# One turned dV or dK tile a block, loads before stores on the queue, and new places for the heads' borrowed-bank work

## The chip, the cores and the metric

The kernel runs on one core of one Trainium2 chip. Time is what the device takes for one execution, in microseconds (us). The times of a kernel are the median of several runs; a profile is one further execution, recorded by the hardware profiler. Times inside a profile are counted from the start of its span.

## The reference, cut to what matters

The reference is a forward pass and its gradient. With `x` of 2048 rows and 576 columns, 32 heads of width 128, and a feed-forward width of 4608, the forward pass is

```python
def _A_ref(x, k_cache, v_cache, wq, wo):
    q = (x @ wq).reshape(B, Sq, H, Dh).transpose(0, 2, 1, 3)
    scores = jnp.einsum("bhqd,bhkd->bhqk", q, k_cache) * (Dh ** -0.5)
    p = _softmax(scores, axis=-1)
    o = jnp.einsum("bhqk,bhkd->bhqd", p, v_cache)
    return o.transpose(0, 2, 1, 3).reshape(B, Sq, H * Dh) @ wo

def _B_ref(x, w_gate, w_up, w_down):
    g = jnp.einsum("bsd,df->bsf", x, w_gate)
    u = jnp.einsum("bsd,df->bsf", x, w_up)
    return jnp.einsum("bsf,fd->bsd", _sigmoid(g) * u, w_down)

xn = _layernorm(x)
out = x + _A_ref(xn, k_cache, v_cache, wq, wo) * _silu(_B_ref(xn, w_gate, w_up, w_down))
```

The kernel returns `out` and, for a given gradient of `out`, the gradients of `x`, `k_cache` (dK), `v_cache` (dV), `wq`, `wo`, `w_gate`, `w_up` and `w_down`. All arrays are bfloat16.

## The kernel before, in words

The work runs through stages on five engines: TensorE (PE) multiplies, VectorE (DVE) and ScalarE (ACT) take results out of the accumulators (PSUM) and do the elementwise work, GpSimd (POOL) does smaller elementwise work and issues DMAs, SyncE (SP) only issues DMAs. What SyncE issues goes out in its program order: an entry that waits holds back all that follow.

- **Feed-forward forward pass** (0 to 463 us): layer norm, gate and up products, down product. Its rows go to scratch arrays in DRAM (`h_d`, `a_d`, `b_d`).
- **Heads** (463 to 3665 us, 32 of them). The order of TensorE, DVE and ACT is written out by hand: every step of a head gets a place on a scale on which one head is 64 places long (`HEAD`), and steps are sorted by place (`at`, `anchor`). The scores of a query tile (`s_half`, two halves of 1024 keys), its exponential on ACT (`s_exp`, L563, a slab `Pq` of 128x2048), the product of dO and V (`dp_half`) and the slab `dSq` fill a head's frame. Each slab is turned by a transposing DMA on SyncE (L600, `PT` and `dST`), except the `dSq` of query tile 9, which TensorE turns in two halves of eight transposes (`trans_pe`, places `DST_PE` after the tile's own). Row products (`row_mm`, L612) read the turned slabs, `kv_mm` (L630) reads slabs as they are and accumulates dV and dK transposed, half of the keys at a time: VA, VB, KA, KB, at places found by filling the frame evenly (`level`), from 24 to 86.7, so into the next head's frame.
- **Borrowed banks.** `ps_acc` has four PSUM banks. `kv_mm` holds two of them for a whole half of the keys (`acckv`), `row_mm` one (`acc`). The rest of the heads' work takes what is left: projections of QT and dOT (`proj`, L511: four chunks of five steps, 0.4 places apart, evicted by ACT) and groups of eight transposes (`pe_transposes`, L518: KT, VT, dOn, Qn and the turned `dSq`, evicted by ACT or DVE). Their places are `QT_AT`, `DOT_AT`, `KT_AT`, `DON_AT`, `VT_AT`, `QN_AT` and `DST_PE` (L684 to L686). QT and KT are those of the next head.
- **Output product and dO** (3665 to 3801 us, L852).
- **Dh stage** (3801 to 4406 us): 18 blocks of 256 feed-forward columns. Per block: dh (L905), `du_blk` and `dg_blk` from it, dWdown (L923), dWup and dWgate (L947, L955). `load_abh(fb + 2)` loads the block after next: `a_blk` and `b_blk` on SyncE (L885), which wait until this block's elementwise work has read their slots, and `h_blk` on POOL. `load_wdT` loads, in pieces, the next third of the turned `w_down`, needed from blocks 6 and 12.
- **c2** (4406 to 4676 us): eight groups of four heads, dWo (L1005) and dWq (L1014, L1023), from `onb` and `dqb`, loaded two groups ahead.
- **c4** (4676 us to the end): the gradient of x, eight groups of 256 rows. Per group eight passes over chunks that transposing DMAs bring (L1061): six chunks `cf` in three slots and two chunks `cq` in two slots.

**The turned tiles.** The heads write dV and dK transposed to DRAM (`dvT_d`, `dkT_d`), 64 tiles of 128x2048 (512 KB each). Later stages turn them back: a transposing DMA loads a tile into SBUF, a plain DMA stores it. `turn(pool, n)` first issues the stores of the tiles loaded last, then loads `n` tiles. Every pool has two slots.

```python
    def turn(pool, n):
        while turned:
            nc.sync.dma_start(*turned.pop(0))
        for _ in range(n):
            if turns:
                ...
                nc.sync.dma_start_transpose(t_[:], src)
```

The dh stage turns two tiles a block (36), c2 two a group (16), c4 the last 12, one in each of passes 1, 4 and 7 of groups 1 to 4.

Of the kernel before, what the change touches and what calls it, by code (L numbers as in the profile page):

```python
# [9 lines left out]
bf = mybir.dt.bfloat16  # L10
# [3 lines left out]
P = 128  # L14
# [81 lines left out]
def kernel(  # L96
# [6 lines left out]
    nc = tc.nc  # L103
    cfg = dict(cfg or {})
    _, S, D = A_x.shape
    _, H, Sk, Dh = A_k_cache.shape
# [3 lines left out]
    NT = S // P  # L110
# [37 lines left out]
    turns = [(src[h], out[0, h].rearrange("(p t) d -> p t d", t=NT)) for h in range(H) for src, out in ((dkT_d, out_2), (dvT_d, out_3))]  # L148
    turned = []

    def turn(pool, n):
        while turned:
            nc.sync.dma_start(*turned.pop(0))
        for _ in range(n):
            if turns:
                src, dst = turns.pop(0)
                t_ = pool.tile([P, NT, P], bf, name="turn")
                nc.sync.dma_start_transpose(t_[:], src)
                turned.append((dst, t_[:]))


# [262 lines left out]
    with tc.tile_pool(name="ld2", bufs=2) as ld2, tc.tile_pool(name="ld1q", bufs=1) as ld1q, \  # L424
# [258 lines left out]
        KVE, OUE = "ss", "s"  # L683
        WOT_AT, DST_PE = 2.0, (6.3, 8.2)  # L684
        QT_AT, DOT_AT = ((41.4, 46.7, 50.0, 53.8), "s"), ((5.6, 8.6, 13.4, 17.4), "s")
        KT_AT, DON_AT, VT_AT, QN_AT = (45.5, 49.2, "s"), (16.2, 25.4, "v"), (29.6, 31.2, "s"), (33.6, 39.4, "s")  # L686
        PSTEP = 0.4
# [101 lines left out]
    if True:  # L789
# [19 lines left out]
        with tc.tile_pool(name="c1b", bufs=1, side="right", reuse_waits="tile") as blk, \  # L809
# [26 lines left out]
            def load_wdT(i, k=0):  # L836
                nc.sync.dma_start_transpose(wdT_h[k][:, i, :], B_w_down[k * FH:(k + 1) * FH, dlo[i]:dlo[i] + P])
# [32 lines left out]
        with tc.tile_pool(name="b1o", bufs=2, reuse_waits="tile") as outp, tc.tile_pool(name="b1k", bufs=2, reuse_waits="tile") as tkp, tc.tile_pool(name="b1t", bufs=3, reuse_waits="tile") as tmpp, \  # L870
# [21 lines left out]
            for fb in range(F // FB):  # L892
# [41 lines left out]
                else:  # L934
                    make_dh()
                    for fl in range(FB // P):
                        make_dwd(fl)
                load_abh(fb + 2)
                if fb < DT * (NWD - 1):
                    load_wdT(fb % DT, 1 + fb // DT)  # L940
                turn(tkp, 2)
                for (blk_, out_, nm) in ((du_blk, out_7, "dwu"), (dg_blk, out_6, "dwg")):
# [16 lines left out]
                for k, out_ in enumerate((out_7, out_6)):  # L959
                    nc.gpsimd.dma_start(out_[D - KL:, fcols], dwl[k * KL:(k + 1) * KL, :])  # L960
            turn(tkp, 0)
        pcw.release()
# [7 lines left out]
        with tc.tile_pool(name="c2b", bufs=1, reuse_waits="tile") as blk, tc.tile_pool(name="c2s", bufs=2, reuse_waits="tile") as sb, \  # L970
# [26 lines left out]
            for hg in range(NHG):  # L997
                cols = slice(hg * HG * P, (hg + 1) * HG * P)
                onb, dqb = held.pop(hg)
                for hl in range(HG):  # L1000
                    h = hg * HG + hl
                    accs = [ps.tile([P, 512], f32, name=f"acc{j}") for j in range(len(ncs))]
                    for st in range(NT):
                        for j, (n0, nn) in enumerate(ncs):
                            nc.tensor.matmul(accs[j][:, :nn], lhsT=onb[:, st, hl * P:(hl + 1) * P], rhs=ds_all[:, st, n0:n0 + nn],  # L1005
                                             start=(st == 0), stop=(st == NT - 1))
                    dwo = sb.tile([P, D], bf, name="dwo")
                    for j, (n0, nn) in enumerate(ncs):
                        alt.copy(dwo[:, n0:n0 + nn], accs[j][:, :nn])
                    nc.gpsimd.dma_start(out_5[h * P:(h + 1) * P, :], dwo[:])  # L1010
# [20 lines left out]
                for (dst, src, d0, kd) in wT_loads[2 * hg:2 * hg + 2]:  # L1031
                    nc.sync.dma_start_transpose(dst[:, :, d0:d0 + kd], src[d0:d0 + kd, :])
                turn(tkp, 2)
            turn(tkp, 0)

# [3 lines left out]
        with tc.tile_pool(name="c4c", bufs=1, reuse_waits="tile") as chp, tc.tile_pool(name="c4s", bufs=2, reuse_waits="tile") as sb, \  # L1039
# [11 lines left out]
            for sbi in range(S // SB2):  # L1051
# [7 lines left out]
                for pi, (src_d, wT, k0, KC, nm) in enumerate(passes):  # L1059
                    ch = chp.tile([P, KC, SB2], bf, name=f"cq{pi % 2}" if nm == "cq" else f"cf{pi % 3}")  # L1060
                    nc.sync.dma_start_transpose(ch[:], src_d[scol, k0 * P:(k0 + KC) * P])  # L1061
                    if sbi == 0 and pi in (1, 3, 4, 6):
                        load_wqT((1, 3, 4, 6).index(pi))
                    elif sbi and pi % 3 == 1:
                        turn(tkp, 1)
                    last = pi == len(passes) - 1
# [7 lines left out]
                for sl in range(nsl):  # L1074
# [23 lines left out]
                    (nc.sync if sbi == NSB - 1 else nc.gpsimd).dma_start(o1[rows, :], dx[:])  # L1098
            turn(tkp, 0)
            assert not turns  # L1100
# [32 lines left out]
```

## Time and profile before

| | us |
|---|---|
| median of 3 runs | 5077.68 (5071.66 to 5115.31) |
| the profiled execution, its own time | 5100.3 |
| its span | 5098.5 |
| TensorE busy | 4977.9 |
| chain that ended last: TensorE / DMA / issue | 86% / 8% / 2% |
| DMA, mean | 212 GB/s |

A line of the profile's groups names line, engine, operation, tiles (out<-in), shapes, count, then busy us and the mean ns of one, then the engine's idle time before it and what ended that. `SPq` is SyncE's queue of DMAs; the time beside an entry is how long SyncE was at it, its landing comes later. A busy TensorE need not be at its peak: a matmul counts as busy from its start to its modelled end, which overlaps the next one's start.

```profile
L612 PE MATMUL acc<-Kn,dST 128*128 128x128 bf16 x8192 | 977.0, 219 | 36.9 <-DMA dST<-dSq 36.2
...
L612 PE MATMUL acc<-Vn,PT 128*128 128x128 bf16 x8192 | 948.8, 219 | 11.7 <-DMA PT<-Pq 11.6
...
L630 PE MATMUL acckv<-Pq,dOn 128*128 128x512 bf16 x2048 | 762.9, 380 | 0.0
```

### The profile page before, as it was taken

Reading aid. Unit: us, or ns where it says so; the run is one execution under the profiler, and the core shown is the slowest. Engines: PE = TensorE matmul, PEld = TensorE weight load, DVE = VectorE, ACT = ScalarE, POOL = GpSimd, SP = SyncE. Lnnn points to the kernel's source line nnn. Section 1 sums busy time; section 2 is a strip of 40 time slices with the busy share of each in tenths; the row PEclk is TensorE's granted clock in tenths of the full one; section 3 lists DMA queues with packets and bytes.
Section 4 is the critical chain, followed back from the end, with each engine's and each line's share of the span. In section 5 each row is a group of like instructions: output and inputs, shape, how many; then the busy total and the mean of one; then the engine's idle time right before and its main releaser. Section 6 shows DMA issues by size and latency. Waiting matters only on the chain.

```text
span 5098.5 us, 103815 instructions
## 1 busy us (share of the span) xinstructions
PE 4977.9 (98%) x43024; PEld 3071.8 (60%) x43024; DVE 3087.7 (61%) x4821; ACT 2435.7 (48%) x3131; POOL 1484.0 (29%) x2197
## 2 busy tenths in 40 slices
PE   9999999999999999999999999999899999899999
PEld 3344666666666666666666666666457777654554
DVE  6556778878887887887888788777432222110101
ACT  5533656666666676666666667666202122100000
POOL 4322323333333333233333323322223223211000
PEclk9999999999999999999999999999999999999999
DMA  7889999999999999999999999999999999999995
GB/s 260 265 206 167 197 198 201 198 197 200 202 200 203 203 201 204 202 203 202 199 200 200 205 204 197 199 199 203 189 235 262 230 244 252 282 278 254 207 198 119
DMA packets 2855051, 1079.04 MB, mean 212 GB/s; under 512 B 2659889, under 2 KB 2782769, under 8 KB 2854577
## 3 DMA queue, kind: packets, MB, share of 16 engines
q1 hardware_dynamic: 2769312, 786.61, 87.3%
q0 software_dynamic: 85264, 285.79, 19.8%
q8 instruction: 336, 5.51, 0.4%
q14 instruction: 139, 1.13, 0.1%
HBM read 172.54 MB, written 234.55 MB: 80 GB/s over the span
## 4 chain that ended last, share of the span: by engine, by line
PE 86%; DMA 8%; issue 2%; DVE 2%; ACT 1%; POOL 1%; SPq 0%; DVEq 0%; POOLq 0%; ACTq 0%
PE acc L612 16%; PE acckv L630 15%; PE sp L552 8%; PE acc L1072 8%; PE dp L582 7%; PE accp L511 5%; PE accw L947 4%; DMA dST<-dSq 4%; PE dh L905 3%; PE acc L392 3%; PE accd L923 3%; PE acc L1005 3%; PE acc L852 2%; PE accq L1014 2%; PE acct L518 2%
## 5 line engine op out<-in xcount | busy, mean ns | idle before, releaser
L563 ACT ACTIVATE Pq<-sneg,nm 128x2048 bf16<-128x2048 bf16 x512 | 1025.0, 2002 | 182.6 <-DVE sneg L554 181.6
L585 DVE SCALAR_TENSOR_TENSOR dSq<-dp,delta,Pq 128x1024 bf16<-128x1024 f32 x608 | 774.9, 1282 | 445.9 <-PE dp L582 442.9
L612 PE MATMUL acc<-Kn,dST 128*128 128x128 bf16 x8192 | 977.0, 219 | 36.9 <-DMA dST<-dSq 36.2
L612 PEld LDWEIGHTS <-dST 128*128 128x128 bf16 x8192 | 692.3, 98 | 464.7 <-DMA dST<-dSq 57.6
L612 PE MATMUL acc<-Vn,PT 128*128 128x128 bf16 x8192 | 948.8, 219 | 11.7 <-DMA PT<-Pq 11.6
L612 PEld LDWEIGHTS <-PT 128*128 128x128 bf16 x8192 | 682.7, 98 | 428.8 <-DMA PT<-Pq 18.6
L630 PE MATMUL acckv<-Pq,dOn 128*128 128x512 bf16 x2048 | 762.9, 380 | 0.0
L630 PE MATMUL acckv<-dSq,Qn 128*128 128x512 bf16 x2048 | 758.9, 379 | 0.0
L554 DVE TENSOR_SCALAR_CACHE_REDUCE sneg<-sp,nm 128x1024 bf16<-128x1024 f32 x512 | 657.0, 1283 | 97.6 <-PE sp L552 64.8
L554 DVE TENSOR_SCALAR_CACHE_REDUCE sneg<-sp 128x1024 bf16<-128x1024 f32 x512 | 625.2, 1221 | 92.2 <-PE sp L552 82.8
L588 ACT ACTIVATE t<-dp,negdelta 128x1024 bf16<-128x1024 f32 x416 | 464.8, 1117 | 426.0 <-PE dp L582 324.5
L552 PE MATMUL sp<-KT,QT 128*128 128x512 bf16 x2048 | 610.5, 380 | 7.3 <-DVE sneg L554 7.0
L582 PE MATMUL dp<-VT,dOT 128*128 128x512 bf16 x2048 | 609.9, 379 | 0.6 <-DVE dSq L585 0.5
L592 DVE TENSOR_TENSOR dSq<-t,Pq 128x1024 bf16<-128x1024 bf16 x416 | 307.3, 739 | 0.0
L571 POOL TENSOR_TENSOR dOn<-dOn,rinv_all 128x256 bf16<-128x256 bf16 x256 | 153.8, 610 | 491.6 <-DVE dOn L42 305.4
L630 PEld LDWEIGHTS <-dOn 128*128 128x128 bf16 x2048 | 200.5, 98 | 74.5 <-issue 0.4
L630 PEld LDWEIGHTS <-Qn 128*128 128x128 bf16 x2048 | 200.5, 98 | 73.8
L511 PE MATMUL accp<-xnT,wq_h 128*128 128x512 bf16 x640 | 240.9, 381 | 2.8 <-ACT xnT L40 0.8
L947 PEld LDWEIGHTS <-xn_all 128*128 128x128 bf16 x2304 | 224.2, 98 | 27.8
L1085 DVE SCALAR_TENSOR_TENSOR junk<-dxn,xn_all 128x576 f32<-128x576 f32 x16 | 12.1, 758 | 369.3 <-ACT dxn L1080 369.3
L676 POOL DMA_DIRECT2D dq_d<-dq_n x128 | 99.1, 774 | 456.6 <-DVE dq_n L675 419.4
L1072 PEld LDWEIGHTS <-cf 128*128 128x128 bf16 x2304 | 146.3, 98 | 141.3 <-DMA cf<-dg_d 3.8
(186 smaller groups left out, 7059.2 us busy)
## 6 DMA issues: line engine op xcount, KB each, us to landing
out_dram<-turn SPq DMA_DIRECT2D x64, 512.0 KB, 4.9
h_d<-h_row POOLq DMA_DIRECT2D x48, 384.0 KB, 3.0
a_d<-a_row POOLq DMA_DIRECT2D x48, 384.0 KB, 3.5
b_d<-b_row POOLq DMA_DIRECT2D x48, 384.0 KB, 4.5
a_blk<-a_d SPq DMA_DIRECT2D x18, 1024.0 KB, 8.3
b_blk<-b_d SPq DMA_DIRECT2D x18, 1024.0 KB, 21.4
du_d<-du_blk POOLq DMA_DIRECT2D x18, 1024.0 KB, 9.6
dg_d<-dg_blk POOLq DMA_DIRECT2D x18, 1024.0 KB, 12.5
```

What stands on the lines that cost most here:

```text
L511: nc.tensor.matmul(acc[:], lhsT=w[:, i, :], rhs=(srcT if i < DL else xnT)[:, i, cs], start=(i == 0), stop=(i == DL))
L552: nc.tensor.matmul(sp[:, c * CH:(c + 1) * CH], lhsT=hs.QT[:, qs], rhs=hs.KT[:, hf * HW_ + c * CH: hf * HW_ + (c + 1) * CH], start=True, st ...
L554: nc.vector.tensor_scalar(sneg[:, hf * HW_:(hf + 1) * HW_], sp[:], -SCALE, None if hf == 0 else nm[:, hf - 1:hf], op0=ALU.mult, op1=ALU.mi ...
L563: nc.scalar.activation(Pq[:], sneg[:], AF.Exp, bias=nm[:, hf:hf + 1], scale=-1.0, accum_out=hs.rs_all[:, qt:qt + 1])
L582: nc.tensor.matmul(dp[:, c * CH:(c + 1) * CH], lhsT=hs.dOT[:, qs], rhs=hs.VT[:, hf * HW_ + c * CH: hf * HW_ + (c + 1) * CH], start=True, s ...
L585: nc.vector.scalar_tensor_tensor(dSq[:, hsl], dp[:], hs.delta[:, qt:qt + 1], Pq[:, hsl], op0=ALU.subtract, op1=ALU.mult)
L588: nc.scalar.activation(t[:], dp[:], AF.Identity, bias=hs.negdelta[:, qt:qt + 1], scale=1.0)
L592: nc.vector.tensor_tensor(dSq[:, hsl], t[:], Pq[:, hsl], op=ALU.mult)
L612: nc.tensor.matmul(bx.acc[:, j, :], lhsT=T[qt][:, kt, :], rhs=getattr(hs, rhs)[:, kt, :], start=(kt == 0), stop=(kt == NT - 1))
L630: nc.tensor.matmul(bx.acc[i][:], lhsT=getattr(hs, rhs)[:, qt, :], rhs=slabs[qt][:, k0:k0 + CH], start=(qt == 0), stop=(qt == NT - 1))
L947: nc.tensor.matmul(acc[:kd, :FB], lhsT=xn_all[:, st, d0:d0 + kd], rhs=blk_[:, st, :], start=(st == 0), stop=(st == NT - 1))
L1072: nc.tensor.matmul(accs[sl][j][:, :nn], lhsT=ch[:, kk, sl * P:(sl + 1) * P], rhs=w_[:, n0:n0 + nn], start=(pi == 0 and kk == 0), stop=(las ...
```

## The change

`turn` now issues the load of one tile first and the store of the tile loaded before it after that. The dh stage turns one tile a block (18 in all), and there the piece of `w_down` goes ahead of the next block's loads. C2 turns one tile after the first head's products and one at the end of each group (16). C4 turns the other 30: one in each of passes 1, 2, 4, 5 and 7 of groups 1 to 6. In the heads the places of `DST_PE`, `QT_AT`, `DOT_AT`, `KT_AT` and `DON_AT` move; as the even filling counts them, the places of VB, KA and KB shift with them.

```diff
-    def turn(pool, n):
-        while turned:
-            nc.sync.dma_start(*turned.pop(0))
-        for _ in range(n):
-            if turns:
-                src, dst = turns.pop(0)
-                t_ = pool.tile([P, NT, P], bf, name="turn")
-                nc.sync.dma_start_transpose(t_[:], src)
-                turned.append((dst, t_[:]))
-
+    def turn(pool, load=True):
+        old, turned[:] = list(turned), []
+        if load and turns:
+            src, dst = turns.pop(0)
+            t_ = pool.tile([P, NT, P], bf, name="turn")
+            nc.sync.dma_start_transpose(t_[:], src)
+            turned.append((dst, t_[:]))
+        for (dst, t_) in old:
+            nc.sync.dma_start(dst, t_)
...
-        WOT_AT, DST_PE = 2.0, (6.3, 8.2)
-        QT_AT, DOT_AT = ((41.4, 46.7, 50.0, 53.8), "s"), ((5.6, 8.6, 13.4, 17.4), "s")
-        KT_AT, DON_AT, VT_AT, QN_AT = (45.5, 49.2, "s"), (16.2, 25.4, "v"), (29.6, 31.2, "s"), (33.6, 39.4, "s")
+        WOT_AT, DST_PE = 2.0, (7.4, 8.7)
+        QT_AT, DOT_AT = ((41.4, 47.2, 55.6, 61.6), "s"), ((5.4, 7.6, 13.6, 17.0), "s")
+        KT_AT, DON_AT, VT_AT, QN_AT = (45.5, 50.2, "s"), (10.9, 25.4, "v"), (29.6, 31.2, "s"), (33.6, 39.4, "s")
...
-                load_abh(fb + 2)
                 if fb < DT * (NWD - 1):
                     load_wdT(fb % DT, 1 + fb // DT)
-                turn(tkp, 2)
+                load_abh(fb + 2)
+                turn(tkp)
...
-            turn(tkp, 0)
+            turn(tkp, False)
...
+                    if hl == 0:
+                        turn(tkp)
                     dwo = sb.tile([P, D], bf, name="dwo")
...
-                turn(tkp, 2)
-            turn(tkp, 0)
+                turn(tkp)
+            turn(tkp, False)
...
-                    elif sbi and pi % 3 == 1:
-                        turn(tkp, 1)
+                    elif sbi and pi % 3:
+                        turn(tkp)
```

More of the change, by code (lines that the diff above doesn't have):

```diff
@@ L1098 @@
                     (nc.sync if sbi == NSB - 1 else nc.gpsimd).dma_start(o1[rows, :], dx[:])
-            turn(tkp, 0)
+            turn(tkp, False)
             assert not turns
```

## The prediction

> **What bounds the kernel now.** The page comes first. TensorE is busy 98% of the span, so a wait of TensorE is worth its own length and everything else is worth what it makes TensorE wait.
> ```profile
> span 5098.5 us, 103815 instructions
> PE 4977.9 (98%) x43024; PEld 3071.8 (60%) x43024; DVE 3087.7 (61%) x4821; ACT 2435.7 (48%) x3131; POOL 1484.0 (29%) x2197
> ```
> Second, busy time by stage: heads, dh stage, dWo/dWq stage (below: c2) and last stage (c4). The columns are the stretch, its length, then busy time of each engine, the granted clock, the DMA share and GB/s. TensorE idles 62 us of 3202 in the heads, 17 in the dh stage, 13 in c2 and 13 in c4.
> ```profile
> 463.00:3665.00 3202.00, 3139.90 (x28551) 1993.93 (x28551) 2541.21 (x3681) 2073.94 (x2368) 1054.11 (x1495) 1.00 1.14 200
> ...
> 3801.00:4406.00 605.00, 587.86 (x5444) 467.54 (x5443) 163.20 (x411) 128.93 (x264) 176.37 (x265) 0.99 1.07 253
> 4406.00:4676.00 270.00, 256.99 (x1840) 131.07 (x1838) 27.83 (x53) 23.85 (x53) 44.44 (x82) 0.97 1.06 283
> 4676.00:5098.50 422.50, 409.79 (x3328) 210.98 (x3328) 50.35 (x128) 14.65 (x65) 17.21 (x32) 0.99 0.86 176
> ```
> Third, the chain of waits in order of time (start, us, what). Outside the heads it leaves TensorE for long only three times after the dh stage has begun, each time for a load that SyncE issued late.
> ```profile
> 3982.07 25.37 DMA wdT<-in_B_w_down_dram
> ...
> 4124.66 27.21 DMA b_blk<-b_d
> ...
> 4406.82 15.60 DMA onb<-on_d
> ```
> Fourth, SyncE's order of time, which shows why that load of wdT was late: two stores, then two turned loads that need the slots of those very stores, and only then the blocks' own loads. The turned pair holds the queue from 3943.57 to 3978.28.
> ```profile
> 3943.57 1.00 SPq L153 DMA_DIRECT2D out_dram<-turn  x2
> 3948.47 13.21 SPq L158 DMA_TRANSPOSE turn<-dkT_d  x1
> 3961.72 16.56 SPq L158 DMA_TRANSPOSE turn<-dvT_d  x1
> 3978.32 0.58 SPq L885 DMA_DIRECT2D a_blk<-a_d  x1
> ```
>
> **Dh stage: -20 us.** Undisturbed, a block takes 32.52 us in the chain (dh of block 3869.00 to 3901.52). From 3966.56 two blocks take 75.74 us, from 4107.40 two take 74.41; against 65.04 that is 10.7 and 9.4, together 20.1, the lower clock after each stall (0.91 to 0.96 in the windows by block) included. With one tile a block, a turned load takes the slot whose store was issued a block before, so it waits for nothing; wdT and the block's loads stand ahead of it; and half of the turned traffic leaves a stage whose DMA share is 1.07. The other queue with loads here, POOL's h_blk, is not touched. What is late next is b_blk, whose load can go out some 10 us into a block and is needed two blocks on; its median landing of 21.4 us is covered. Bounds: -22 and -12 (one stall stays, smaller).
>
> **Start of c2: -13 us.** TensorE waits 13.0 us for onb, and the first head's 128 matmuls take 17.57 us where later heads take 15.79: 14.8. The load is issued at 4406.82 because the last turns hold SyncE from 4366 to 4406; its slot lies on loads of the last two blocks, which TensorE last reads at 4393.6. Issued there it lands before TensorE's last dh work ends at 4409.4. Next late is dqb, whose slot waits for the store of dwl (issue at 4415.78, 6.4 us after that end) and whose transfer took 12.7 us beside others: needed 15.8 us after the end, it may cost 0 to 3, I take 1.5. Bounds -15 and -5. The turns inside c2 stay two to a group, beside the same work, and the tail of turns ahead of c4's first loads stays about as long: 0.
>
> **Heads, waits removed: -17 us.** The page's idle times hide these, because a matmul's 164 ns of pipeline covers them. In the order of time they show:
> ```profile
> 1927.92 1.01 ACT L40 COPY KT<-acct 128x1024 bf16<-128x1024 bf16 x1 [1.12 <-PE acct L518]
> ```
> ```profile
> 1928.32 0.59 PE L582 MATMUL dp<-VT,dOT 128*128 128x512 bf16 x2
> 1928.98 0.38 PE L511 MATMUL accp<-xnT,wq_h 128*128 128x512 bf16 x1
> ```
> 512-wide matmuls start 0.216 us apart and 128-wide ones 0.055. Two from 1928.32 reach 1928.75, but the next starts at 1928.98, when the KT copy has given its bank back: 0.23 us. The first dOT projection after the dOn copy loses 0.26 likewise (copy ends 1978.24, matmul 1978.29, due 1978.03). Over 31 heads: 15; KT's first transposes behind the QT copy, 0.09 by start distances, bring it to 17. The new places (a head is 64 places, 3202/32/64 = 1.56 us each) put 1.4 to 2.7 between these, where there are 0.8 to 1.2 now, and a third of a place is enough.
>
> **Heads, waits added: +44 us.** Four accumulation banks: two for acckv, one for acc, one left to borrow. First, the third QT projection is now at 55.6 and its last step at 57.2, and the TensorE transposes of dSq at 57.4 (before: 55.4 and 56.3). In the built order of the changed kernel two 128-wide matmuls stand between. The bank comes free after matmul 0.38, handover 0.04, QT copy 0.585 and handover 0.05 = 1.06 us; the order covers 0.216 + 2 x 0.055 = 0.33. Wait 0.73 x 31 heads = 22.6. The second half of those transposes follows 1.3 places later instead of 1.9, and ACT's dST copy (1.00 us) starts late itself: 0.1 x 31 = 3. Second, dOT's first two projections move from 5.6 and 8.6 to 5.4 and 7.6. The second half of dK opens its two banks there (about 6.8 and 7.7, by the same even filling), and in the built order its second bank now comes behind the first matmul of dOT's second projection, which has taken the last one. So it waits for dOT's first copy, and that stands behind an exponential:
> ```profile
> 1960.89 2.02 ACT L563 ACTIVATE Pq<-sneg,nm 128x2048 bf16<-128x2048 bf16 x1
> 1962.79 0.20 ACT L563 ACTIVATION_READ_ACCUMULATOR Pq<-sneg,nm 128x1 f32 x1
> 1962.88 0.58 ACT L40 CAST dOT<-accp 128x512 bf16<-128x512 f32 x1
> ```
> The fourth query tile's second score pair starts at 1961.72 in that head, so the bank is free 1.80 us after it (1963.46 and handover). The built order puts after that pair's start 4 matmuls of 512 and 6 of 128, 1.19 us. Wait 0.61 x 31 = 18.9. Bounds: 0.2 each if ACT happened to be free at once, 2 if it had just begun an exponential; I take the places, since ACT's order is written out by hand. ACT and TensorE themselves do the same work.
>
> **Heads, slabs that land late: -4 us.** The page gives 36.2 and 11.6 us before L612 for dST and PT, 12.7 of it at the very end, behind oT's load on SyncE; that order is the same in the built program. Of the other 35, some goes under the new waits, which lie between a slab's end and its use for about a third of the tiles; bounds -20 and +5. Heads together: -17 + 44 - 4 = +23, between +8 and +35.
>
> **C4: +6 us.** Thirty turned tiles instead of 12: five in each of groups 1 to 6. A group takes TensorE 50.6 us (361.6 us for 1488 of the 208 steps of a group each). SyncE's issue, medians from groups with turns: chunk 3.6 x 6, dq chunk 4.78 x 2, together 31.2; a turned tile 3.2 and its store 0.57, five times 18.9. That makes 50.0, so two of three spare microseconds per extra tile are gone; and turns that follow each other by one chunk wait for a store (3.5 us or more to land): about 1. I take 1 us a group, 6; bounds 0, and 20 if every issue grows by 8%. The page DMA: Bandwidth & Descriptors of the Trainium skill (Latency and other measured facts) gives DMA transposes 261 GB/s with a strided middle dimension; 9.44 MB a group would then need 36 us, c4 would cost 0 and the sum be -10. Here SyncE, without a pause from 4804.71 to 4836.69, moved 6.29 MB of transposes beside two stores, 197 GB/s; that row decides.
>
> **Sum.** -20 - 13 + 23 + 6 = -4. Against the profiled execution's 5100.3: 5096. It lay 22.6 over the median of the runs shown (5077.68, from 5071.66 to 5115.31), so for the median: 5074.
>
> **Rivals.** One: c4 fills the DMA engines and comes out slower. By windows, the share is 0.98 with three tiles a group (4740 to 4920) and 0.69 without (4960 to 5060), so 0.097 x 50.6 = 4.9 us a tile, and 0.69 x 50.6 + 5 x 4.9 = 59.4 with five. If 1.02, the share of c4's first 53 us, in which SyncE issues almost without pause, is full, a group takes 58.2 us: 6 x 7.6 = +46 in place of +6, and the time is 5114, slower than before. It decides as soon as a group passes 50.6. Against it: the heads run at 1.14, where it would be 52.1 and +9. Chance 0.12. Two: the new waits in the heads cost nothing, because slabs land late anyway; then -17 stands alone there, sum -44, time 5034. Against it: at most 35 us are such waits, and at other places of the head. Chance 0.12. Three: SyncE's queue was not the cause; the dh and c2 loads are late from full DMA engines, and both stalls stay: +23 + 6 = +29, time 5107. For it: that turned load took 16.56 us to issue. Against it: the median of such loads in that stage is 2.6 to 3.1 us, and half of the turned traffic goes. Chance 0.13. The forecast has 0.63, with a range of its own of 5052 to 5096.
>
> **Numbers.** About 1% (51 us) is what a measurement here can tell from no change. The range takes in the forecast, rival three and the lower half of rival one: 5048 to 5114. Faster by over 1% is part of rival two (0.04), slower by over 1% the upper part of one and a little of three (0.05); the rest is 0.91.
>
> **What would show it.** In the profile of the changed kernel: blocks of 32.5 us throughout the dh stage; no onb wait; in each head a QT copy that ends right as the transposes of dSq start, and an acckv matmul starting right as a dOT copy ends; groups of c4 at 50.6 to 52 us. Heads shorter than 3202 us would make it wrong on the low side, groups of 55 us or more on the high side.

## The result and the profile after

The changed kernel takes 5130.55 us (median of 13 runs, 5109.88 to 5166.18); the kernel before, run 13 times beside it, 5111.34 (5071.66 to 5129.41). The medians lie 19 us apart, the means 31; the ratio, which is that of the means, is 1.0061 [1.0032, 1.0089]. So it is some 31 us slower, within the 1% that the prediction called no change, but outside its range, and up where it said 4 us down.

The profiled execution is 5123.3 us against 5100.3. The page's first lines of the changed kernel answer to those of before:

```profile
span 5121.5 us, 103036 instructions
...
PE 4945.9 (97%) x42269; PEld 3076.6 (60%) x43024; DVE 3080.8 (60%) x4821; ACT 2453.1 (48%) x3131; POOL 1487.6 (29%) x2197
```

Here 755 matmul records are missing (43024 weight loads stand beside 42269 matmuls), so busy TensorE is read too low. Stage lengths are safe: each is cut from the first matmul of a stage to the first of the next. The windows of the changed kernel, cut so (heads, output product called c1 here, dh stage to the first matmul on `onb`, c2, c4; columns as in the prediction):

```profile
461.30:3689.20 3227.90, 3120.01 (x28033) 2001.07 (x28577) 2535.12 (x3682) 2090.57 (x2368) 1059.74 (x1499) 1.00 1.14 199
3689.20:3829.40 140.20, 130.81 (x1078) 69.28 (x1099) 47.86 (x74) 7.87 (x31) 32.78 (x61) 0.99 1.18 193
3829.40:4417.00 587.60, 584.32 (x5445) 467.93 (x5480) 163.59 (x412) 129.16 (x263) 177.56 (x267) 1.00 0.97 236
4417.00:4670.80 253.80, 249.37 (x1763) 127.48 (x1793) 27.36 (x52) 23.85 (x53) 43.36 (x80) 1.00 1.03 274
4670.80:5114.40 443.60, 417.00 (x3261) 213.30 (x3328) 46.87 (x120) 13.58 (x61) 17.21 (x32) 0.97 1.05 213
```

The same cut for both kernels, and for a second profile of each, taken in the experiments:

| us | heads | c1 | dh and start of c2 | c2 | c4 |
|---|---|---|---|---|---|
| before | 3206.7 | 131.4 | 621.0 | 253.4 | 415.5 |
| before, second profile | 3216.1 | 139.9 | 624.8 | 254.2 | 416.6 |
| changed | 3227.9 | 140.3 | 587.5 | 253.8 | 443.6 |
| changed, second profile | 3237.7 | 141.3 | 587.4 | 264.1 | 441.2 |

Three stages moved most, and in this pair of profiles the first two did what was forecast (c1's 9 us are taken up in run 15). **The dh stage** lost its stalls. In the chain of waits of the changed kernel (start, us, what) its blocks follow each other at 32.52 us, and no load stands before the first product on `onb` (L1004):

```profile
3961.68 8.84 PE dh L904 x80
...
3994.20 8.84 PE dh L904 x80
...
4026.72 8.84 PE dh L904 x80
...
4415.16 1.87 PE accl L954 x32
...
4417.43 2.61 PE acc L1004 x20
```

**The heads** got the two new waits at the places foretold. In the changed kernel's order of time, the transposes of dSq start as the QT copy ends, and `acckv` starts as the dOT copy ends, which stood behind an exponential:

```profile
1952.63 0.38 PE L510 MATMUL accp<-xnT,wq_h 128*128 128x512 bf16 x1
...
1953.04 0.59 ACT L40 CAST QT<-accp 128x512 bf16<-128x512 f32 x1 [0.85 <-PE accp L510]
1953.68 0.61 PE L517 MATMUL acct<-ident,dSq 128*128 128x128 bf16 x8 [0.56 <-ACT QT L40]
...
1973.76 2.02 ACT L562 ACTIVATE Pq<-sneg,nm 128x2048 bf16<-128x2048 bf16 x1
...
1975.75 0.58 ACT L40 CAST dOT<-accp 128x512 bf16<-128x512 f32 x1
1976.39 0.38 PE L629 MATMUL acckv<-dSq,Qn 128*128 128x512 bf16 x1 [0.44 <-ACT dOT L40]
```

By the distances of matmul starts the first cost 22.5 us in 31 heads and the second 18.8; the old waits behind KT's and dOn's copies are gone. ("Bank wait" below means this: a matmul that waits until a copy has given its accumulation bank back. A "late slab" is a turned slab that lands after TensorE is ready for it.)

**C4** is the surprise. Its groups took 58.6 and then seven times 51.0 us before; now 65.5, 51.2, 56.8, 52.0, 60.3, 51.9, 54.9 and 50.9. The chain there runs through SyncE's queue and ends at a chunk that lands late:

```profile
4922.54 2.98 SPq L1062
...
4925.57 1.99 SPq L156
...
4927.61 0.58 SPq L159
...
4928.23 9.67 DMA cq<-dq_d
...
4937.94 0.66 PE acc L1073 x2
```

A chunk, a turned load (L156) and a store (L159) are issued without a pause, and the `cq` chunk asked for behind them lands 9.67 us later, with TensorE waiting.

### The profile page after: what moved, and what is told of

Read it like the earlier page. It is cut to its first block, busy times and chain, and to the rows that moved or that the text cites. A ratio compares the mean times of both kernels' runs of the same rounds, so it can differ in the third digit from the quotient of the medians.

```text
span 5121.5 us, 103036 instructions
## 1 busy us (share of the span) xinstructions
PE 4945.9 (97%) x42269; PEld 3076.6 (60%) x43024; DVE 3080.8 (60%) x4821; ACT 2453.1 (48%) x3131; POOL 1487.6 (29%) x2197
## 4 chain that ended last, share of the span: by engine, by line
PE 73%; ACT 9%; DMA 9%; DVE 4%; issue 3%; SPq 2%; DVEq 0%; ACTq 0%; POOL 0%; POOLq 0%
PE acc L611 13%; PE acckv L629 12%; PE dp L581 6%; ACT Pq L562 5%; PE acc L1073 5%; PE accw L946 5%; PE sp L551 5%; DMA dST<-dSq 4%; PE accp L510 4%; PE dh L904 3%; DVE sneg L553 3%; PE acc L391 3%; PE accd L922 3%; PE g_ps L294 2%; PE acc L1004 2%
## 5 line engine op out<-in xcount | busy, mean ns | idle before, releaser
L611 PE MATMUL acc<-Kn,dST 128*128 128x128 bf16 x8192 | 972.7, 219 | 33.4 <-DMA dST<-dSq 24.6
L611 PE MATMUL acc<-Vn,PT 128*128 128x128 bf16 x8192 | 952.2, 219 | 21.2 <-DMA PT<-Pq 12.4
L629 PE MATMUL acckv<-dSq,Qn 128*128 128x512 bf16 x1921 | 715.1, 380 | 17.1 <-ACT dOT L40 13.7
L629 PE MATMUL acckv<-Pq,dOn 128*128 128x512 bf16 x1888 | 704.4, 380 | 5.0
L551 PE MATMUL sp<-KT,QT 128*128 128x512 bf16 x1952 | 589.2, 380 | 9.8 <-DVE sneg L553 7.9
L581 PE MATMUL dp<-VT,dOT 128*128 128x512 bf16 x1920 | 581.9, 379 | 1.3
L510 PE MATMUL accp<-xnT,wq_h 128*128 128x512 bf16 x608 | 229.6, 382 | 1.0 <-ACT xnT L40 0.8
```

The lines of the kernel that those rows point to most:

```text
L510: nc.tensor.matmul(acc[:], lhsT=w[:, i, :], rhs=(srcT if i < DL else xnT)[:, i, cs], start=(i == 0), stop=(i == DL))
L551: nc.tensor.matmul(sp[:, c * CH:(c + 1) * CH], lhsT=hs.QT[:, qs], rhs=hs.KT[:, hf * HW_ + c * CH: hf * HW_ + (c + 1) * CH], start=True, st ...
L581: nc.tensor.matmul(dp[:, c * CH:(c + 1) * CH], lhsT=hs.dOT[:, qs], rhs=hs.VT[:, hf * HW_ + c * CH: hf * HW_ + (c + 1) * CH], start=True, s ...
L611: nc.tensor.matmul(bx.acc[:, j, :], lhsT=T[qt][:, kt, :], rhs=getattr(hs, rhs)[:, kt, :], start=(kt == 0), stop=(kt == NT - 1))
L629: nc.tensor.matmul(bx.acc[i][:], lhsT=getattr(hs, rhs)[:, qt, :], rhs=slabs[qt][:, k0:k0 + CH], start=(qt == 0), stop=(qt == NT - 1))
```

## Experiments

The theory: the heads lose by the two bank waits, the dh stage gains because SyncE's queue is freed, c4 loses because five turned tiles a group are more than SyncE's queue carries in 51 us. The rivals are named in each expectation. Totals of two kernels carry an interval of about +/- 12 us, so most verdicts rest on stage lengths, and those come from one profile of each kernel.

**1. The places alone** (the turns as before)

```diff
-        WOT_AT, DST_PE = 2.0, (6.3, 8.2)
...
+        WOT_AT, DST_PE = 2.0, (7.4, 8.7)
+        QT_AT, DOT_AT = ((41.4, 47.2, 55.6, 61.6), "s"), ((5.4, 7.6, 13.6, 17.0), "s")
+        KT_AT, DON_AT, VT_AT, QN_AT = (45.5, 50.2, "s"), (10.9, 25.4, "v"), (29.6, 31.2, "s"), (33.6, 39.4, "s")
```

> The kernel before with only the new places of the heads' borrowed work; the turns are as before. My theory is that the 21 us which the heads lost come from two bank waits that the new places make (transposes of dSq behind the QT copy, 0.73 us in 31 heads; acckv behind the dOT copy, 0.61 us in 31 heads) less the three old waits that are gone. Then heads 3228 us (+/- 3), the stages from dh on as before (dh to onb 621, c2 253, c4 415), total +20 to +23 us. Rival A: the new places also make c1's loads of oT late; then c1 is 140 us and not 131, total +30. Rival B: the heads' loss came from the chip's run and not from the places; then heads 3207 and total 0.

Measured: ratio 1.0024 [1.0003, 1.0044]; heads 3220.8 us, with 22.5 us of `acct<-ident,dSq` behind the QT copy and 19.0 of `acckv` behind the dOT copy; c1 139.6, dh 623.3, c4 414.7. The waits are made by the places. The heads' length and the total (12 us over before, 20 to 23 were expected) fell short, because late slabs took only 39 us here against 56 before.

**2. The turns alone** (the changed kernel with the places of before)

```diff
-        WOT_AT, DST_PE = 2.0, (7.4, 8.7)
+        WOT_AT, DST_PE = 2.0, (6.3, 8.2)
...
```

> The changed kernel with the old places in the heads; only the turns are new. My theory: heads 3207 us, dh with the start of c2 588 (-33 against before), c4 443 (+28: group 0 about 65 us, groups 1 to 6 with five turned tiles 52 to 60, group 7 without any 51), total between -8 and +2 us against before. Rival A (c1's late loads come from the new places): c1 131. Rival C (they come from chance or from the turns): c1 140 again, total up to +5.

Measured: 1.0022 [0.9999, 1.0045], 11 us slower where -8 to +2 was expected; heads 3214.5, c1 134.7, dh 601.1 (two slow blocks, below), c4 445.0. So the turns by themselves are no gain: what dh gives, c4 takes back. The two halves add up, within their intervals, to the whole.

**3. Three turned tiles a group in c4**

```diff
                 turn(tkp)
+                if fb % 2:
+                    turn(tkp)
...
-                    elif sbi and pi % 3:
+                    elif sbi and pi % 3 == 1:
```

> Old places in the heads; the turn is the new one (load first, store of the tile before last), with one tile in even and two in odd blocks of dh (27), two in each part of c2 as in the changed kernel (16) and three in each of c4's groups 1 to 7 (21). My theory: three turned tiles a group fit in SyncE's time, so c4's groups 1 to 7 take 51.0 us each; group 0 takes 65 again, since the last tiles at c2's end are still ahead of its first chunk; c4 about 422. In dh the even blocks run without a wait, the odd ones wait at most as before, dh with the start of c2 588 to 605. Total -10 to -26 us against before. Rival (c4's loss is not one of tiles in a group): groups 1 to 6 stay at 52 to 60 and the total is no lower than that of the kernel with five a group.

Measured: 1.0024 [1.0005, 1.0043]. C4's groups 1 to 7 are 50.9 to 51.0 us each, as expected; group 0 is 68.4, dh 605.9. The total missed: heads 3222.6 us in this profile, with the code of before. That the heads of one code vary by 20 us was the lesson here: in ten profiles with the places of before they take 3203 to 3225 us, 3215 on the mean. The limit of c4 lies above three tiles a group.

**4. C4's turned tiles on ScalarE's queue**

```diff
-            nc.sync.dma_start_transpose(t_[:], src)
+            q.dma_start_transpose(t_[:], src)     # c4: q = nc.scalar
...
-            nc.sync.dma_start(dst, t_)
+            q.dma_start(dst, t_)
```

> The changed kernel (new places, five tiles a group in c4), with the turned tiles of c4 issued, loads and stores, by ScalarE and not by SyncE. Theory, SyncE's time to issue is what runs out in c4: with five of 13 transfers taken away from SyncE the groups 1 to 6 go back to 51 to 52 us, c4 to about 422, total 20 to 25 us under the changed kernel, so about +8 against before. Rival, the DMA engines are full with five tiles a group: the groups stay at 54 to 57 us on the mean, c4 440 to 447, total as the changed kernel (+25 to +35 against before).

Measured: 1.0297 [1.0267, 1.0327], and no answer to the question. ScalarE ran its 30 turned tiles from the end of c2 into group 1, ahead of the first groups' copies; groups 0 and 1 took 134.0 and 102.0 us, the later ones, with none, 51.0. The chain of this kernel shows why so long: turned tile and chunk alternate, each issued when the other queue's transpose has landed.

```profile
4733.09 5.74 DMA cf<-du_d
...
4738.90 4.34 DMA turn<-dkT_d
...
4743.29 5.28 DMA cf<-dg_d
...
4748.65 4.97 DMA turn<-dvT_d
```

As built, transposing DMAs of two queues do not overlap, so a second queue gives them no second lane.

**5. One of the two bank waits undone**

```diff
-        QT_AT, DOT_AT = ((41.4, 47.2, 55.6, 61.6), "s"), ((5.4, 7.6, 13.6, 17.0), "s")
+        QT_AT, DOT_AT = ((41.4, 47.2, 55.6, 61.6), "s"), ((5.4, 7.2, 13.6, 17.0), "s")
```

> The changed kernel with one number of the heads' new places put 0.4 us earlier (the second of dOT's four places: 7.2 and not 7.6); turns and all other places as in the changed kernel. My theory: the wait of acckv<-dSq,Qn behind the dOT copy (18.8 us in 31 heads) was made by that one place alone; it goes, and the rest of the heads stays, so the heads take 3228 - 19 = 3209 us (3200 to 3215, since dp's waits of 6 us may shift too), and the total is 19 us (10 to 26) under the changed kernel, so +5 to +20 against before. The wait of acct<-dSq behind the QT copy stays at 22 us. Rival: the places are coupled, and the wait turns up at another bank: heads 3220 to 3235.

Measured: 1.0042 [1.0016, 1.0069]; heads 3223.5. The wait of `acckv` is gone (the group of this kernel ends in an idle time of 1.9 us), that of `acct` still 22.5. But the slabs land later: by the group lines 42.3 and 10.9 us are ended by dST and PT, where the changed kernel has 24.6 and 12.4.

```profile
L611 PE MATMUL acc<-Kn,dST 128*128 128x128 bf16 x8192 | 974.7, 220 | 52.8 <-DMA dST<-dSq 42.3
L611 PE MATMUL acc<-Vn,PT 128*128 128x128 bf16 x8192 | 956.2, 219 | 19.4 <-DMA PT<-Pq 10.9
...
L629 PE MATMUL acckv<-dSq,Qn 128*128 128x512 bf16 x1923 | 716.6, 381 | 1.9 <-issue 0.2
```

Of 19 us taken away, 4 were left in the stage. The expectation fell (3200 to 3215 us), though with one profile and a spread of 20 us the 4 itself says little.

**6. Store first in dh, one tile a block**

```diff
-                turn(tkp)
+                turn(tkp, first=True)     # stores of the tile before, then the load
```

> Old places in the heads; turns as in the changed kernel, but in dh the store of the tile before goes ahead of the load again (one tile a block stays). If it is the amount that freed the queue: blocks of 32.5 us with at most one or two slow ones, no wait for onb, dh with the start of c2 588 to 602, total as with the turns alone (+5 to +15 against before). If it is the order (a store that waits for its tile holds up the block loads behind it): the waits of before are back, dh with the start of c2 612 to 625, total +20 to +30.

Measured: 1.0036 [1.0010, 1.0061]; dh and start of c2 597.4 us, no wait for `onb`. With load first, eleven profiles of one tile a block gave 587.3 to 609.8, mean 592.6; with two tiles and store first, three gave 621.0, 623.3 and 624.8. The one slow block of this run, 42.3 us, holds a stall of 8.0 us behind a late instruction packet (last section); without it the stage would have the 587 us of the best runs with load first. In all twelve profiles with one tile a block no block waits more than 0.6 us for a load. In runs 3, 13 and 14, which also have the piece of `w_down` ahead but turn a second tile in some blocks, waits of 2.4 to 9.8 us behind `b_blk` are back. So the number of tiles a block decides, and neither the order of load and store nor the place of `w_down`.

**7. C4's stores on GpSimd's queue**

```diff
-            nc.sync.dma_start(dst, t_)
+            (q or nc.sync).dma_start(dst, t_)     # c4: q = nc.gpsimd
```

> Old places in the heads; turns as in the changed kernel, but c4's 30 stores of turned tiles go out on GpSimd's queue, their loads stay on SyncE. Bytes and transposes are the same. If SyncE's time to issue is what runs out: five stores of 0.59 us and the waits between them less a group, SyncE's share of issuing goes from 0.97 to about 0.91, groups 1 to 6 at 51 to 52.5 us on the mean (55 with the turns alone), c4 425 to 432, total 12 to 20 us under the turns alone. If the DMA engines or the memory are full: groups stay at 54 to 56 us, c4 440 to 448. If the long part is the issue of the transposes themselves: something between, 52.5 to 54.

Measured: 1.0014 [0.9988, 1.0041]; groups 1 to 6 at 53.7 us on the mean, c4 442.0: the middle outcome of the expectation. SyncE is rid of the stores, its share of issuing in these groups falls from 0.97 to 0.93, and 0.8 us a group is gained: the stores' issue is not the limit.

**8. A first mended version**

```diff
-        QT_AT, DOT_AT = ((41.4, 47.2, 55.6, 61.6), "s"), ((5.4, 7.6, 13.6, 17.0), "s")
+        QT_AT, DOT_AT = ((41.4, 47.2, 52.0, 54.2), "s"), ((5.4, 7.2, 13.6, 17.0), "s")
...
-                    if hl == 0:
+                    if hl == 0 and hg < NHG - 1:
...
-                turn(tkp)
+                if hg < NHG - 1:
+                    turn(tkp)
...
-                    elif sbi and pi % 3:
+                    elif pi in {0: (5, 7), NSB - 1: (0, 1, 2, 3, 4, 5)}.get(sbi, (1, 2, 4, 7)):
```

> The version I now think best: dh one tile a block, load first (18); c2 two a part but none in the last part (14), so that c4's first chunks are asked for earlier; c4 two in group 0, four a group in 1 to 6, six early in group 7 (32). In the heads the new places with three numbers changed (second dOT 7.2, third and fourth QT 52.0 and 54.2), which should take both new bank waits away and bring back none of the old. My theory: heads 3185 to 3197 us, dh with the start of c2 588 to 602, c4 group 0 53 to 58 us, groups 1 to 7 51.0 to 51.5 us (four a group need a share of 0.89 of SyncE's time), c4 412 to 420; total 35 to 60 us under before. Rival (c4's loss starts at any tile above three): groups 1 to 6 at 53 us or more, c4 430. Rival (places coupled): heads 3207 or more, total -15 to -35.

Measured: 0.9996 [0.9969, 1.0023]. Groups 1 to 6 with four tiles: 51.4 and five times 51.0; group 0, with two, 62.2. The last, with six in a row, took 59.6. Both new bank waits are gone and no old one is back (9 us of bank waits in all), and yet the heads take 3231.1 us, where 3185 to 3197 was expected: the waits ended by slabs are 57.0 and 17.3 us.

```profile
L611 PE MATMUL acc<-Kn,dST 128*128 128x128 bf16 x8192 | 996.0, 220 | 67.8 <-DMA dST<-dSq 57.0
L611 PE MATMUL acc<-Vn,PT 128*128 128x128 bf16 x8192 | 962.6, 219 | 26.1 <-DMA PT<-Pq 17.3
```

This profile lies 32 us over the median of its runs, and c1 took 156.9 us in it, waiting for loads of `oT`; so its heads may be longer than this kernel's usually are. By the ratios this kernel lies some 33 us under the changed one (+/- 20), of which c4 explains 15.

So a new theory for the heads: the transposing slab loads set the pace (SyncE is issuing DMAs for 0.96 of the stage, slabs for 0.95, without a difference between kernels), and a bank wait mostly gives them time that they would take anyway.

**9 and 10. The slabs copied plainly**, once with the changed kernel's places and once with those of run 8. The transposition of the slabs is left out, so these two kernels do not compute the reference's dWq.

```diff
-            nc.sync.dma_start_transpose(t_tile(T, qt, name)[:], slabs[qt][:])
+            nc.sync.dma_start(t_tile(T, qt, name)[:], slabs[qt][:].rearrange("p (t d) -> p t d", t=NT))
```

> The changed kernel with the heads' 992 transposing slab loads (PT and dST) made plain copies of the same bytes, so the transposition of P and dS is left out in 31 and 30 of 32 heads' slabs that go by DMA, and dV, dK and dQ are not the reference's. A plain copy of that size is issued in 0.4 to 0.6 us and not in 3.1. If the slab queue (SyncE issues transposes for 0.96 of the heads' time) takes up what the bank waits leave, late slabs go (45 us in the changed kernel) and both new bank waits stay at their full 22 and 19 us: heads 3180 to 3190 us. Rival (late slabs come from the engines that make the slabs): slab waits stay near 45 us, heads 3220 or more.

> As the run before (plain slab copies, same parts left out), with the heads' places of the best version so far, which have neither of the two new bank waits. Theory of the exchange (with transposing slabs a microsecond of bank wait taken away comes back as late slabs, since the queue sets the pace): with plain copies it is paid out in full, heads 3140 to 3155 us, 35 to 45 us under the run before, while with transposing slabs the same pair of places gave 3228 and 3231. Rival (bank waits are worth little in any case): under 15 us between the two.

Measured: heads 3176.2 us with the changed places and 3132.2 with the mended ones, both a little under what was expected, and 44.0 apart, as expected. The windows over the heads, first of run 9, then of run 10:

```profile
460.90:3637.10 3176.20, 3107.93 (x28033) 1999.92 (x28577) 2534.83 (x3682) 2088.67 (x2367) 1059.02 (x1499) 1.00 0.55 201
```

```profile
460.70:3592.90 3132.20, 3096.31 (x28039) 1995.92 (x28576) 2541.26 (x3682) 2075.19 (x2367) 1056.23 (x1497) 1.00 0.56 204
```

With slabs on time (1 us of slab waits and none) the bank waits are paid in full, 50 against 8 us. The same two sets of places were 3228 and 3231 us with transposing loads. The share of the DMA engines, 1.14 in every other run, is 0.55 at the same bytes, so whether SyncE's issue or those engines are the limit is not told apart: a transposing load takes both.

Run 4's kernel has the changed places too: 48 us of bank waits, 37 of late slabs, heads 3217. Both kinds of wait by the distances of matmul starts (the page's idle times are smaller, since a matmul's modelled end covers part of them):

| heads, us | bank waits | late slabs | length |
|---|---|---|---|
| before, two profiles | 21, 22 | 56, 57 | 3207, 3216 |
| changed, two profiles | 50, 49 | 45, 57 | 3228, 3238 |
| places alone (1) | 49 | 39 | 3221 |
| one wait undone (5) | 32 | 63 | 3224 |
| both undone (8) | 9 | 88 | 3231 |
| plain slabs (9, 10) | 50, 8 | 1, 0 | 3176, 3132 |

In the ten profiles with the places of before late slabs take 47 to 69 us, 58 on the mean, and in the four with the changed places 37 to 57, 44 on the mean. So the 88 us with both waits undone stand out from either, and 14 of the 28 us of new bank waits are covered by slabs that would have been late.

**11. C4's turned loads made plain** (their transposition is left out)

```diff
-            nc.sync.dma_start_transpose(t_[:], src)
+            nc.sync.dma_start(t_[:], src.rearrange("p (t d) -> p t d", t=NT))     # in c4
```

> Old places in the heads, turns as in the changed kernel, but c4's 30 loads of tiles are plain loads of the same bytes (their transposition is left out, so most of the tiles of dV and dK that c4 writes are not turned). Stores stay. If it is the transposing loads' long issue on SyncE that makes groups 1 to 6 long (five of 2.7 us): 51.0 to 51.5 us each. If it is the bytes that the engines of the DMA move (5 x 1 MB a group in and out): 53 us or more on the mean, as with the turns alone (54.5).

**12. C4's stores left out** (those tiles of dV and dK aren't written)

```diff
-        old, turned[:] = list(turned), []
+        old, turned[:] = ([] if keep else list(turned)), []     # c4: keep
```

> Old places in the heads, turns as in the changed kernel, but c4's 30 stores of turned tiles are left out (those tiles of dV and dK are not written); the transposing loads stay. If the issue of 13 transposes a group (8 x 4.2 + 5 x 2.7 = 47 us of 51) is what fills SyncE: groups 1 to 6 stay at 52.5 to 54.5 us on the mean. If the stores' bytes slow the transposes down: issue of a chunk back to 3.5 us, groups 51.0 to 51.5 us.

Measured: both bring groups 1 to 6 to 50.96 us each. So neither theory holds alone. The windows over groups 1 to 6 (the last three columns are clock, DMA share and GB/s), in turn for three tiles a group (run 3), for four (the last version, below), for five (run 2), for five with plain loads and for five without stores:

```profile
4745.80:5051.50 305.70, 305.70 (x2498) 158.06 (x2497) 37.65 (x97) 10.70 (x48) 12.89 (x24) 1.00 0.99 210
```

```profile
4721.90:5027.70 305.80, 305.80 (x2499) 157.83 (x2498) 37.73 (x97) 10.71 (x48) 12.89 (x24) 1.00 1.09 231
```

```profile
4735.00:5062.30 327.30, 313.34 (x2498) 159.76 (x2497) 37.73 (x97) 10.71 (x48) 12.90 (x24) 0.98 1.10 232
```

```profile
4738.60:5044.30 305.70, 303.08 (x2447) 157.84 (x2496) 37.65 (x97) 10.72 (x48) 12.89 (x24) 1.00 1.07 249
```

```profile
4710.30:5016.00 305.70, 303.08 (x2447) 157.68 (x2496) 37.64 (x97) 10.73 (x48) 12.89 (x24) 1.00 0.98 199
```

Read the last column. From three to four tiles it grows by 21 GB/s at the same length; from four to five it stays at 231 to 232, and the length grows instead. Five tiles in 51 us would need 232 x 54.55 / 50.96 = 248 GB/s, and 249 are moved when the turned loads are plain. So over these six groups the mix of transposes and stores is full at about 232 GB/s. SyncE shows it as longer issue: on the mean a chunk takes it 3.33 us with five tiles and no stores, 3.93 with three tiles (run 3), 4.16 with four (run 14) and 4.3 with five. That also explains run 7: moving the stores to another queue leaves the bytes, and at 235 GB/s the groups stay long though SyncE's queue has room. Single groups do pass with five tiles in 51.2 us; whether the next ones pay for it wasn't traced.

**13 and 14. Versions within these limits**: places of before; dh 22 tiles (a second one in blocks 2, 5, 12, 15), c2 14 (none in the last part), c4 none in group 0 and four in each other group. In run 14 the last group's passes are 1, 2, 4, 5 and 7 in place of 0, 1, 2, 3 and 5; the last of them only stores.

```diff
+                if fb in (2, 5, 12, 15):
+                    turn(tkp)
...
+                    elif pi in {0: (), NSB - 1: (0, 1, 2, 3, 5)}.get(sbi, (1, 2, 4, 7)):
```

> Old places in the heads; turns load first, store last: in dh one tile a block and a second in four of 18 blocks (22), in c2 two a part but none in the last (14), in c4 none in group 0, four in each of groups 1 to 7 (28). The runs so far say that dh gains 20 to 33 us with one tile a block, that c4 keeps 50.96 us a group up to four tiles, and that the heads are best left alone. So dh with the start of c2 590 to 605, c4's group 0 58 to 63 us, groups 1 to 7 51.0 us, heads 3205 to 3225 (they vary by that much from run to run with the same code), total 10 to 30 us under before (ratio 0.994 to 0.998). Rival (what dh gains comes back as late loads elsewhere): c1 or c4's group 0 longer by as much, ratio 0.999 to 1.002.

> As the version before it, but the four tiles of c4's last group stand at its chunks 1, 2, 4 and 5 and not at 0, 1, 2 and 3. There the last group took 58.4 us, with waits of 3.0 and 2.4 us for chunks that were asked for behind four turned tiles in a row. If it was that density: the last group 51 to 52 us, c4 416 to 419, total 15 to 32 us under before (ratio 0.994 to 0.997). Rival (the last group is long because its tiles come on top of something else): 57 to 60 us again, ratio 0.998.

Measured: 0.9979 [0.9954, 1.0004] and 0.9979 [0.9953, 1.0006]; for run 14 0.994 to 0.997 was expected. Run 13's dh took 610.5 us (590 to 605 was expected), with two waits for `b_blk`. The last group was 58.4 us in run 13 and 50.9 in run 14, so it was the density: four turned loads behind four chunks in a row. Run 14's stages are 3217.6, 137.6, 593.7, 252.9 and 415.9 us, c4 with group 0 at 59.0. It keeps dh's gain and pays nothing in c4; its median is 15.6 us under that of before run beside it, but the interval still touches no change.

**15 and 16. Both kernels once more**

> The kernel before once more, nothing changed, for the spread of its stages. If c1's 9 us more in the changed kernel are the run's and not the change's: c1 between 133 and 140 here too (131 in the first profile). If they are the change's: 130 to 132. Heads 3200 to 3222, dh with the start of c2 615 to 625, c4 415.

> The changed kernel once more, nothing changed. Heads 3218 to 3232 with bank waits of 49 us, dh with the start of c2 587 to 602, c4 441 to 446 with groups 1 to 6 at 54 to 55 us on the mean; c1 133 to 140.

Measured: the second rows of the table of stages. C1 is 139.9 us in the unchanged kernel too, so its 9 us were the run's: 131.4 is the shortest c1 of all eighteen profiles. The changed kernel's bank waits, dh and c4 repeat; its heads are 6 us over the range expected, c2 is longer by 10, and at its end TensorE waits 12.3 us for c4's first chunk. The chain there:

```profile
4679.27 0.33 SPq L159
...
4679.65 11.17 DMA cf<-du_d
...
4690.86 14.57 PE acc L1073 x96
```

SyncE had finished the last store of c2's turned tiles at 4679.60, and only then asked for the chunk.

## Why the prediction was wrong, step by step

- **The base.** "For the median: 5074" took 22.6 us off because the profiled execution lay that far over the median of three runs. Over 13 runs the median of before is 5111, and the profiled execution lies 11 us under it. This alone is 34 us of the miss. Three runs between 5072 and 5115 did not fix the base to better than these 34 us, and the range had no term for it.
- **Dh stage -20 and start of c2 -13.** Right: -33.5 in the first pair of profiles, -37.4 in the second. Rival three falls in its outcome, that both stalls stay: with one tile a block they go, in whichever order (run 6). Whether it was SyncE's queue that was freed, as the prediction has it, or the DMA engines isn't told apart, since one tile fewer a block eases both.
- **Heads +23.** The two waits were right, foretold as 22.6 and 18.9 us and measured as 22.5 and 18.8, and the pairs show +21.2 and +21.6. That the sum came out so near is in part luck: over all profiles the heads take 3226 us with the changed places (four) and 3215 with the old ones (ten), 11 us apart, give or take some 10. That is inside the bounds of +8 to +35, and late slabs gave back some 14 us instead of the 4 in the sum. What the term had wrong is that its parts stand side by side. Late slabs and bank waits exchange, in part at least: in one profile each, undoing one wait of 19 us gave 4 and undoing both gave nothing, while with plain slabs the same waits cost 44. Rival two ("the new waits cost nothing, because slabs land late anyway") had the mechanism and the wrong place for its argument: 35 us of late slabs are not the most that can be covered, since more come when the waits go.
- **C4 +6.** Here the sum failed: "I take 1 us a group, 6". Groups 1 to 6 cost 3.6 us each, 21 together. The issue times were medians of groups with three tiles, and they grow with the traffic: six chunks of 4.3, two of 5.4, five times 2.8 and 0.6 make 53.6 us and not 50.0. The bound of 20 was reached, though not as "if every issue grows by 8%" has it: chunks grew by a fifth, a turned tile's issue shrank from 3.2, and the sum grew by 7%. Of run 2's 21.5 us, by the windows, 14.0 are idle and 7.5 are matmuls at a lower clock.
- **"The tail of turns ahead of c4's first loads stays about as long: 0."** Also failed. The changed kernel has TensorE there earlier and SyncE 3 us later (first chunk asked for at 4663.19, before at 4660.12). Group 0 took 6.9 us more, 4.1 in the second pair, where another 12.3 were waited ahead of it. Without turned tiles in c2's last part (run 14) it takes 59.0.
- **Rival one** named the mechanism, DMA engines that are full, but priced it at 46 us by a share of 1.02 as full. The share reached 1.10, and with that its own sum, 59.4 / 1.10, gives 54.0 us a group and +20, close to the 54.5 and 21 measured.
- **C1** wasn't in the sum; its 9 us are chance (run 15).

In the first pair of profiles the stages sum up: 21.2 + 8.9 - 33.5 + 0.4 + 28.1, and 2.1 less ahead of the heads, make the 23.0 us between the two executions.

## What to carry to other kernels

Issue times of DMAs read from one traffic hold for that traffic only: add the bytes of the stage, and compare with the highest rate that any stretch of the same kind of transfers has reached. Before taking a wait away, ask what else in that stage is busy for 0.96 of the time; taking away a wait that only covers for it may pay little. And moved work should be spread to the count at which nothing grows (here four turned tiles a group, one a block, none just ahead of a stage's first loads).

## What the runs showed that was not expected

**A short stall costs about one and a half times its length.** TensorE waited 2.2 us for a chunk in run 2; the windows after it (matmuls, clock, DMA share, GB/s) show the clock at half for most of 4 us, 3.4 us by the trace's own clock records:

```profile
4880.00:4882.00 2.00, 0.55 (x5) 1.00 0.75 168
4882.00:4884.00 2.00, 2.00 (x13) 0.64 1.06 199
4884.00:4886.00 2.00, 2.00 (x9) 0.51 1.15 261
4886.00:4888.00 2.00, 2.00 (x17) 1.00 1.08 118
```

22 matmuls in 4 us where some 34 would go, so about 1.4 us more are lost. Over the six groups the 14.0 us of idle time became 21.5. The Trainium skill (TensorE: Matmul & The Clock Gate, Part 1) says that an idle window of about 3.4 us drops the clock to half and a busy one restores it. The half clock and its length agree; here a wait of 2.2 us was enough.

**A transposing DMA is not as cheap as a plain one.** For the same 0.5 MB from SBUF to SBUF SyncE needs 3.1 us against 0.47, and the DMA engines' share in the heads is 1.14 against 0.55 (runs 9 and 10). The Trainium skill (Advanced Engine Details and Errata, X-Bar Transpose (TRN2)) says that on this chip they are as fast as regular ones; these runs say otherwise. The 261 GB/s for transposes of the Trainium skill (DMA: Bandwidth & Descriptors, Latency and other measured facts), which the prediction set aside, is near what SyncE issues when no store stands beside them: 0.786 MB in 3.33 us is 236 GB/s, and 184 with five tiles and their stores (4.27 us).

**TensorE can stand still because its instructions come late.** In run 2's dh stage two blocks were slow without a releaser. These windows of run 2 show TensorE nearly idle from 4145, while the DMA engines' share is at its highest and little is moved:

```profile
4140.00:4145.00 5.00, 5.00 (x55) 4.36 (x52) 1.57 (x5) 2.13 (x4) 0.00 (x0) 1.00 1.15 72
4145.00:4150.00 5.00, 0.67 (x7) 0.35 (x4) 1.47 (x4) 0.58 (x1) 0.00 (x0) 0.87 1.54 94
```

The idle time of 6.65 us is put down to issue: nothing that the profile's semaphores show ended it. But the trace also holds the DMA packets that bring instructions (q8 of the page, 16 KB each). None started between 4120.44 and 4149.52; that one ended at 4150.66, and TensorE went on at 4152.32. The dh stages of all eighteen profiles have 17 stalls of over 0.6 us without a releaser. Each ends 1.3 to 1.7 us after such a packet, and ahead of each packet lie 22 to 30 us without one, where about 14 are usual; only 3% of the stage's time lies so behind a packet. So instructions that come late are the cause, and with the half clock behind each stall they make the spread of the dh stage from 587 to 610 us with one tile a block. Why the packets come late isn't shown; DMA engines at a share of 1.54 would fit.
